# A fused attention, expert and dense kernel: results stored out of another tile, a third bank in the last layer, one more weight split early

## The chip, the cores and the metric

The kernel runs on one core of a Trainium2 chip. The metric is the device time of one execution in microseconds (us); for each kernel the median of several executions is given. A core has five engines that run their own instruction streams beside each other: PE (matrix products), DVE (vector), ACT (scalar), POOL (GpSimd) and SP (which here issues nearly all DMAs). They wait for each other by semaphores.

## The reference

```python
# 1. attention, 2 batches x 8 heads x 768 positions x 64, only between
#    positions whose query and key fall into the same of 64 hash buckets
# 2. experts: x is [1536, 512]; each token goes to 2 of 8 experts
h = np.maximum(x[mask] @ w1[e], 0.0)                 # w1 [8, 512, 1024]
out[mask] += top2_w[mask, k, None] * (h @ w2[e])     # w2 [8, 1024, 512]
# 3. dense layer
h = x @ w_in                                         # [512, 2048]
g = h - np.tanh(h)
return (g @ w_out).astype(np.float32)                # [2048, 512]
```

The result has shape [1536, 512]. The weights of the dense layer come in 64-bit form and are turned into float32 inside the kernel.

## The kernel before, in words

The attention fills the first third of the span; from there on PE does the products of the experts and of the dense layer.

**Products in parts.** Each operand of a product is split into a high part, which PE takes at its faster float type, and a low part, the remainder. A product is three matmuls: high by high, high by low, low by high (L1068 to L1070 for the first product of an expert, L1093 to L1095 for the second). `split_w` makes the parts of a weight tile `wt` out of a raw tile `wraw`: ACT copies the high part (L851), then the low part is a subtraction (L850), on POOL in two halves for experts 0, 1 and 7, on DVE in one piece for the others. In the last layer DVE does it in two halves, which wait in a list `later` and are taken out one by one around a step's other work.

**Segments.** `segs` lists the expert work: segments 0 and 1 are expert 0, one for each batch (240 rows of tokens, two row blocks of 120); segments 2 to 7 are experts 1 to 6 (448 rows, three blocks and a tail); segments 8 and 9 are expert 7 (240 rows each). The main loop goes over segments 1 to 9; a segment has eight steps f, one for each 128 columns of w1. In a step PE does the first product of the next step (`h_step`), ACT and DVE turn its bank into `hh` and `hl` (relu, high and low: L1084, L1086), and PE then does the second product of this step into banks that stay open over the whole segment (`y_step`). After the last step `y_out` copies these banks to a tile in SBUF (DVE L1125, ACT L1123), and the store to the DRAM tensor `Y` (L1126) goes out at the next `store()`.

**What holds the order.** The order on each engine is the one in which the code is written. In a step the loop does: `store()`; as many `fetch()` as the depth allows (a DMA from DRAM into a raw tile: L876 and L878 for experts, L874 from `W2f` for the dense layer); `load_x` (L1048, L1051: token rows of the next segment from `Xg`); `trans_x` (PE transposes the token rows L1061, ACT and DVE make high part `xh` and low part `xl`: L1062, L1063); and `next_w`, the split of one weight tile, in the steps that a table names (`LASTW` in the last segment).

**Tiles.** `stg` has two raw tiles `wraw`; a fetch or a result that wants one waits until the last reader of that tile is done. The tiles `xh` and `xl` of a segment come from `mx[n % 2]`: even and odd segments have one set each. The last layer's rows (block 0 to 3 of 384 rows) use the same two sets.

**The conditional.** In segment 1 all engines read a count (L1256) and jump past a block that handles experts with too many tokens (`tc.If`, L1257). With these inputs the block is not entered.

**The last layer.** It has 4 blocks of 16 steps. `h2_step` does the first product into a bank of group "b", ACT forms the square and the tanh (L1368 to L1375), POOL one subtraction (L1374), DVE three steps of a polynomial (L1379, L1381, L1383; the last one reads the bank and so frees it), a predicated copy (L1393) and the low part (L1399). `o2_step` does the second product. `combine` turns the next block's rows (L1350) into banks of group "a" and writes `xh` and `xl` (L1352, L1353); for block 0 this happens in the last segment. A bank is one of eight of 2 KB per partition; a product waits until the last reader of its bank is done.

Of the kernel before, what the change touches and what calls it, by code (L numbers as in the profile page):

```python
# [6 lines left out]
F32 = mybir.dt.float32  # L7
# [13 lines left out]
PF = 3  # L21
# [14 lines left out]
CAP = 448  # L36
# [4 lines left out]

LASTV = (0, 2, 3, 4, 5, 6)

LASTW = (2, 3, 5, 7)

WARM = (7, 1, 2, 10)

# [29 lines left out]
def body(tc, q, k, v, proj, w_gate, w_noise, noise, w1, w2, w_in, w_out, out):  # L77
    nc = tc.nc
    PS = bass.MemoryType.PSUM
    B, H, S, D = q.shape  # L80
# [4 lines left out]
    DM = H * D  # L85
    KD4 = DM // 128
# [13 lines left out]
    with ExitStack() as ctx:  # L100
# [6 lines left out]
        stg = pool("stg", 2)  # L107

        banks = dict(BANKS)
        nbank = dict.fromkeys(banks, 0)  # L110

        def bank(tag):
            r = banks[tag]
            nbank[tag] += 1
            n = r[nbank[tag] % len(r)]
            return psp.tile([128, 512], F32, tag=f"b{n}", name=f"bank{n}")
# [720 lines left out]
        rings = {}  # L837
# [24 lines left out]
        wsrc = [(e, f) for e in range(E) for f in range(NF)] + [("m", f) for f in range(NF2)]  # L862
        wn = [0]
        rings["A"] = wA

        fn, RAW = [0], {}
# [125 lines left out]
        for g in range(NI // 2):  # L992
# [14 lines left out]
            b, P = divmod(g, NP)  # L1007
# [27 lines left out]
        def blocks(n):  # L1035

            rows, nb = segs[n][3:]
            m = min(rows // nb, 128)
            return m, rows - nb * m
# [74 lines left out]
        def y_out(n):  # L1114
            e, b, r0, rows, nb = segs[n]
            m, tail = blocks(n)
            if nb == 2:
                yo = stg.tile([128, 2, DM], F32, name="wraw")
            else:
                yo = mm[n % len(mm)].tile([128, 4, DM], F32, name="xy")  # L1120
            for j, ps in enumerate(YP[n][:nb]):
                if j % 2:
                    nc.scalar.activation(yo[:m, j], ps[:m], AF.Copy)  # L1123
                else:
                    nc.vector.tensor_copy(yo[:m, j], ps[:m])  # L1125
            stores.append(lambda: nc.sync.dma_start(out=Y[r0:r0 + nb * m].rearrange("(p j) d -> p j d", j=nb), in_=yo[:m, 0:nb]))  # L1126
            if tail:
                ps = YP[n][nb]
                nc.scalar.activation(yo[:tail, nb], ps[64:64 + tail], AF.Copy)
                nc.vector.tensor_tensor(yo[:tail, nb], ps[:tail], yo[:tail, nb], op=ALU.add)  # L1130
                stores.append(lambda: nc.sync.dma_start(out=Y[r0 + nb * m:r0 + rows], in_=yo[:tail, nb]))
# [38 lines left out]
        mm, mx = {}, {}  # L1170
# [34 lines left out]
        last = NI - 1  # L1205
# [112 lines left out]
        BC = TB // 128  # L1318
# [22 lines left out]
        def combine(t0):  # L1341

            blk, j = divmod(t0, BC)
            if j == 0:
                XH2[blk] = mx[blk % 2].tile([128, KD4, CAP], F32R, name="xh")
                XL2[blk] = mx[blk % 2].tile([128, KD4, CAP], F32R, name="xl")
            u = hd["g", t0][:, 0]
            ps = bank("a")
            for dc in range(KD4):
                nc.tensor.transpose(ps[:, ck(dc)], u[:, ck(dc)], ident)  # L1350
            p3 = ps.rearrange("p (c n) -> p c n", c=KD4)
            nc.scalar.activation(XH2[blk][:, :, ck(j)], p3, AF.Copy)  # L1352
            later.insert(0, lambda: nc.vector.tensor_tensor(XL2[blk][:, :, ck(j)], p3, XH2[blk][:, :, ck(j)].bitcast(F32),  # L1353
                                                            op=ALU.subtract))
# [76 lines left out]
        NSG = len(segs)  # L1431
        for n in range(1, NSG):
            last = n == NSG - 1
            if n == NSG - B:
                rings["C2"] = ctx.enter_context(tc.tile_pool(name="wC2", bufs=WC2, reuse_waits="tile"))
                store()
                mid.close()
                del rings["st"]
                rings["C"] = ctx.enter_context(tc.tile_pool(name="wC", bufs=WC, side="right", reuse_waits="tile"))
            if last:  # L1440
                store()
                m2 = ctx.enter_context(tc.tile_pool(name="m2", bufs=2, side="right", reuse_waits="tile"))
                gb2 = m2.tile([128, 1], F32, name="gb2")
                nc.vector.memset(gb2, G2 / (2 * G3))
                gsb = m2.tile([128, 1], F32, name="gsb")
                nc.vector.memset(gsb, -GS)
            fx = 0 if n == B - 1 else 1
            for f in seg_steps(n, None if last else n + 1):
                if (n, f) == (1, IFS):
                    sched.close()  # L1450
                    overflow()
                    manual()
                store()
                while fn[0] < min(wn[0] + (PF if "st" in rings else 1), len(wsrc)):
                    fetch()
                if not last and f == fx:
                    load_x(n + 1)
                for dc in range(0 if last else KD4):
                    if f == (5 + dc // 2 if n == B - 1 else 3 + dc):
                        trans_x(n + 1, dc)  # L1460
                if (1, CV1 + 4) <= (n, f) < (NSG - B, 0):
                    convert_more(CVN)
                if (1, CV1) <= (n, f) < (NSG - B, 0):
                    while conv64 and len(RAW64) + (hd.get("cv") is not None) < 2:
                        fetch64(conv64.pop(0))
                if segs[n][1] in (None, B - 1) and (f in LASTW if last else n >= B or f >= W1) or n == NSG - B and f in LASTV:
                    next_w()
                if B <= n < B + WN0 - NF and f == 4:
                    next_w()
                for j in range(BC if last else 0):  # L1470
                    if f == 1 + j // 2:
                        gather(j)
                    if f == 4 + j:
                        combine(j)
                        flush(1)
                    if f == 3 + j:
                        mix(j)
                        flush(1)
        store()
        hd["second"] = True  # L1480
        done = -1
        for n in range(-LA, len(steps2)):
            la = LA + (LAE if n + LA >= len(steps2) - 2 else 0)
            while done < min(n + la, len(steps2)):
                done += 1
                h2_step(at(done), at(done - 1))
            blk, f = at(n + LA) or (NBK, 0)
            for j in range(BC if blk + 1 < NBK else 0):
                t0 = (blk + 1) * BC + j
                if f == 3 + 2 * j:  # L1490
                    gather(t0)
                if f == 9 + j:
                    mix(t0)
                if f == 11 + j:
                    combine(t0)
            if n >= 0:
                flush(max(0, len(later) - 2))
                next_w()
                o2_step(*steps2[n])
# [30 lines left out]
```

## Time and profile before

| | us |
|---|---|
| median of 3 runs | 928.76 |
| lowest and highest of the runs | 925.42, 929.61 |
| the profiled execution | 933.93 |
| its span | 932.1 |
| PE busy in it | 897.7 |

The span is what the trace covers; the profiled execution lasts 1.83 us longer than its span, and is 5.17 us above the median of the runs. In the rows further down, a time at the start of a row is in us from the start of the span. Square brackets at the end of a row tell how long the engine sat idle before that instruction and what ended the idle time: an engine, the tile, and the line; "SPq" and "ACTq" are an engine's own sequencer.

### The profile page before, as it was taken

Reading aid. Unit: us, or ns where it says so; the run is one execution under the profiler, and the core shown is the slowest. Engines: PE = TensorE matmul, PEld = TensorE weight load, DVE = VectorE, ACT = ScalarE, POOL = GpSimd, SP = SyncE. Lnnn points to the kernel's source line nnn. Section 1 sums busy time; section 2 is a strip of 40 time slices with the busy share of each in tenths; the row PEclk is TensorE's granted clock in tenths of the full one; section 3 lists DMA queues with packets and bytes.
Section 4 is the critical chain, followed back from the end, with each engine's and each line's share of the span. In section 5 each row is a group of like instructions: output and inputs, shape, how many; then the busy total and the mean of one; then the engine's idle time right before and its main releaser. Section 6 shows DMA issues by size and latency. Waiting matters only on the chain.

```text
span 932.1 us, 13632 instructions
## 1 busy us (share of the span) xinstructions
PE 897.7 (96%) x4736; PEld 699.3 (75%) x4736; DVE 677.7 (73%) x1290; ACT 539.9 (58%) x1039; POOL 372.8 (40%) x325
## 2 busy tenths in 40 slices
PE   8999999998997788999999999999999999999998
PEld 3555555554556677888888888888889899989997
DVE  7788787889757325797887878665888677677665
ACT  7658666864453133444444444454777777777765
POOL 6687778875667443000000004602342342342221
PEclk9999999999999899999999999999999999999999
DMA  5635553300222478686858777555420110110000
GB/s 123 171 117 170 159 182 106 103 24 7 93 64 95 163 222 256 218 287 214 271 199 292 236 255 248 174 197 179 135 69 1 57 46 1 57 46 1 35 1 34
DMA packets 104625, 123.72 MB, mean 133 GB/s; under 512 B 32121, under 2 KB 75177, under 8 KB 104553
## 3 DMA queue, kind: packets, MB, share of 16 engines
q1 hardware_dynamic: 100712, 110.23, 37.6%
q0 software_dynamic: 3840, 12.59, 4.0%
q8 instruction: 38, 0.62, 0.3%
q14 instruction: 35, 0.28, 0.1%
HBM read 82.79 MB, written 37.72 MB: 129 GB/s over the span
## 4 chain that ended last, share of the span: by engine, by line
PE 55%; DVE 3%; ACT 1%; DMA 1%; issue 1%; POOL 0%; DVEq 0%; SPq 0%; POOLq 0%
PE bank L1068 9%; PE bank L1070 9%; PE bank L1069 9%; PE bank L1095 8%; PE bank L1094 8%; PE bank L1093 8%; PE bank L1110 2%; PE bank L1061 1%; DVE g_u L1381 1%; PE bank L1350 1%; DMA xy<-Xg 1%; DVE wt L850 1%; DMA Y<-xy 0%; DVE hh L1399 0%; DVE g_u L1383 0%
## 5 line engine op out<-in xcount | busy, mean ns | idle before, releaser
L1068 PE MATMUL bank<-xh,wt 128*128 128x384 f32 (+2 forms) x544 | 186.3, 342 | 4.8 <-DVE g_u L1383 2.8
L1069 PE MATMUL bank<-xl,wt 128*128 128x384 f32 (+2 forms) x544 | 183.1, 337 | 0.0
L1070 PE MATMUL bank<-xh,wt 128*128 128x384 f32 (+2 forms) x544 | 183.1, 337 | 0.0
L1093 PE MATMUL bank<-wt,hh 128*128 128x512 f32 (+1 forms) x400 | 159.6, 399 | 9.5 <-ACT hh L1084 6.1
L850 POOL TENSOR_TENSOR wt<-wraw,wt 128x512 fp32r<-128x512 f32 x48 | 68.5, 1451 | 246.8 <-ACT wt L851 234.7
L1095 PE MATMUL bank<-wt,hh 128*128 128x512 f32 (+1 forms) x400 | 159.3, 398 | 0.1
L1094 PE MATMUL bank<-wt,hh 128*128 128x512 f32 (+1 forms) x400 | 158.9, 397 | 0.0
L1374 POOL TENSOR_TENSOR g_th<-g_h,g_th 128x384 f32<-128x384 f32 x64 | 67.2, 1050 | 187.2 <-ACT g_th L1373 186.7
L450 ACT ACTIVATE p<-bank 128x384 f32<-128x384 f32 x192 | 91.8, 489 | 72.1 <-PE bank L449 66.1
L415 DVE TENSOR_REDUCE mx<-bank 128x1 f32<-128x384 f32 x192 | 103.3, 551 | 31.1 <-PE bank L414 29.0
L1068 PEld LDWEIGHTS bank<-xh,wt 128*128 128x128 f32 x544 | 102.5, 188 | 13.9 <-DVE g_u L1383 4.8
L1069 PEld LDWEIGHTS bank<-xl,wt 128*128 128x128 f32 x544 | 102.5, 188 | 6.7 <-DVE xl L1353 0.2
L851 ACT ACTIVATE wt<-wraw 128x1024 fp32r<-128x1024 f32 x80 | 84.2, 1054 | 36.4 <-PE bank L1110 20.5
L1070 PEld LDWEIGHTS bank<-xh,wt 128*128 128x128 f32 x544 | 102.4, 188 | 3.1
L1093 PEld LDWEIGHTS bank<-wt,hh 128*128 128x128 f32 (+1 forms) x400 | 75.6, 189 | 22.9 <-ACT hh L1084 6.4
L483 POOL TENSOR_TENSOR ps<-ps,p 128x768 f32<-128x768 f32 x47 | 85.9, 1827 | 11.7 <-ACT p L450 7.1
L1095 PEld LDWEIGHTS bank<-wt,hh 128*128 128x128 f32 (+1 forms) x400 | 75.5, 189 | 18.3 <-DVE hh L1399 0.6
L1084 ACT ACTIVATE hh<-bank 128x448 fp32r<-128x448 f32 (+1 forms) x80 | 37.7, 473 | 83.6 <-PE bank L1070 34.9
L1086 DVE SCALAR_TENSOR_TENSOR hh<-bank,hh 128x384 fp32r<-128x384 f32 (+2 forms) x128 | 45.8, 388 | 54.7 <-ACT hh L1084 46.0
L1094 PEld LDWEIGHTS bank<-wt,hh 128*128 128x128 f32 (+1 forms) x400 | 75.5, 189 | 12.8
L474 PE MATMUL bank<-p,v 128*64 128x384 f32 x384 | 83.8, 515 | 0.0
L448 PE MATMUL bank<-qc,kb 108*128 108x384 f32 (+1 forms) x192 | 79.2, 412 | 1.8 <-DVE qc L438 1.6
(250 smaller groups left out, 1629.4 us busy)
## 6 DMA issues: line engine op xcount, KB each, us to landing
wraw<-in_moe_w_dram SPq DMA_DIRECT2D x128, 256.0 KB
cv_t<-in_moe_w_in_dram SPq DMA_DIRECT2D x16, 512.0 KB
cv_t<-in_moe_w_out_dram SPq DMA_DIRECT2D x16, 512.0 KB
W2f<-cv_w SPq DMA_DIRECT2D x16, 512.0 KB
wraw<-W2f SPq DMA_DIRECT2D x16, 512.0 KB
Xg<-zero SPq DMA_DIRECT2D x14, 512.0 KB
Y<-zero SPq DMA_DIRECT2D x9, 512.0 KB
xy<-Xg SPq DMA_DIRECT2D x6, 768.0 KB
```

The costliest lines, as they stand in the source:

```text
L415: nc.vector.tensor_reduce(MX[i % 2][:, c, hf:hf + 1], ps[:, :HF], op=ALU.max, axis=AX.X)
L448: nc.tensor.matmul(ps[:, :HF], KB[sn(g, par)][r, ck(kc)], QC[sn(g, par)][r, half(hf)], start=True, stop=False)
L450: nc.scalar.activation(hd["p", i, kc][:, half(hf)], ps[:, :HF], AF.Exp, scale=float(D) ** -0.5)
L474: nc.tensor.matmul(hd["o", i][hf * D:(hf + 1) * D, :HF], raw["v", g][:, par, kc], hd["p", i, kc][:, half(hf)], start=(kc == 0), stop=(kc = ...
L483: eng.tensor_tensor(t, hd["p", i, 0] if kc == 1 else t, hd["p", i, kc], op=ALU.add)
L851: nc.scalar.activation(t[:, 0], r, AF.Copy)
L1068: nc.tensor.matmul(ps[:, :n], ws(0, dc), xh[:, dc, :n], start=(dc == 0), stop=False)
L1069: nc.tensor.matmul(ps[:, :n], ws(0, dc), xl[:, dc, :n], start=False, stop=False)
L1070: nc.tensor.matmul(ps[:, :n], ws(1, dc), xh[:, dc, :n], start=False, stop=(dc == KD4 - 1))
L1093: nc.tensor.matmul(ps[:m], a, t[:, 0, 1], start=first, stop=False)
L1094: nc.tensor.matmul(ps[:m], a, t[:, 1, 1], start=False, stop=False)
L1095: nc.tensor.matmul(ps[:m], l, t[:, 0, 1], start=False, stop=last)
```

## The change

There are five edits:

1. `y_out` of a segment with two row blocks (0, 1, 8 and 9) no longer takes a raw tile from `stg`. It takes the buffer of the segment's own low part, `xl` of `mx[n % 2]`, of which the last reader is the segment's last first product.
2. `LASTW` names one more step, 6, so that five weight tiles of the last layer are split in the last segment, and one fewer in the last layer's first block.
3. In the last segment the fetch depth is 2 instead of 1 from step 3 on.
4. In segment 8 the token rows of segment 9 are transposed at steps 4, 5, 6, 6 instead of 3, 4, 5, 6.
5. In the last layer, group "a" is bank 1 and group "b" banks 2, 3 and 0, until the first `combine` of that layer (block 1's, row tile `t0 == BC`); from there "a" is banks 0 and 1 and "b" banks 2 and 3, as before.

```diff
-LASTW = (2, 3, 5, 7)
+LASTW = (2, 3, 5, 6, 7)
...
             if nb == 2:
-                yo = stg.tile([128, 2, DM], F32, name="wraw")
+
+                yo = mx[n % 2].tile([128, KD4, CAP], F32, name="xl")
+                yo = yo.rearrange("p c n -> p (c n)")[:, 0:2 * DM].rearrange("p (j d) -> p j d", j=2)
...
-                while fn[0] < min(wn[0] + (PF if "st" in rings else 1), len(wsrc)):
+                while fn[0] < min(wn[0] + (PF if "st" in rings else 2 if last and f >= 3 else 1), len(wsrc)):
                     fetch()
...
-                    if f == (5 + dc // 2 if n == B - 1 else 3 + dc):
+                    if f == (5 + dc // 2 if n == B - 1 else min(4 + dc, 6) if n == NSG - 2 else 3 + dc):
                         trans_x(n + 1, dc)
...
         hd["second"] = True
+
+        banks.update(a=[1], b=[2, 3, 0])
+        nbank["b"] %= 2
...
                 if f == 11 + j:
+                    if t0 == BC:
+                        banks.update(a=[0, 1], b=[2, 3])
+                        nbank.update(a=0, b=min(nbank["b"] % 3, 1))
                     combine(t0)
```

The lines behind `y_out` stand two lines further down in the changed kernel (the store L1126 is L1128 there, the jump L1257 is L1259).

**SP around the conditional, in segments 0 and 1.** `wraw` are the weight fetches, `xy<-Xg` the loads of token rows, `Y<-` the store of segment 0's result. Before:

```order
L878 DMA wraw<-in_moe_w_dram 128x512
L1256 TENSOR_LOAD cmi
L1256 ISA x2
L1048 DMA xy<-Xg 120x1024
L876 DMA wraw<-in_moe_w_dram 128x4x128
L1126 DMA Y<-wraw 120x1024
L878 DMA wraw<-in_moe_w_dram 128x512
L1048 DMA xy<-Xg 128x1536
L1051 DMA xy<-Xg 128x512
L876 DMA wraw<-in_moe_w_dram 128x4x128
L878 DMA wraw<-in_moe_w_dram 128x512
L1257 COMPARE_AND_BRANCH
```

After:

```order
L878 DMA wraw<-in_moe_w_dram 128x512
L876 DMA wraw<-in_moe_w_dram 128x4x128
L878 DMA wraw<-in_moe_w_dram 128x512
L876 DMA wraw<-in_moe_w_dram 128x4x128
L878 DMA wraw<-in_moe_w_dram 128x512
L1258 TENSOR_LOAD cmi
L1258 ISA x2
L1048 DMA xy<-Xg 120x1024
L1048 DMA xy<-Xg 128x1536
L1128 DMA Y<-xl 120x1024
L1051 DMA xy<-Xg 128x512
L1259 COMPARE_AND_BRANCH
```

Two weight fetches, of two DMAs each, that stood behind the reading of the count now stand ahead of it; between the load of token rows and the store of the result no weight fetch is left.

**DVE in the first steps of the last layer** (numbers behind names tell buffers apart; `bank3_7244` is a tile in bank 3). Before, the fourth and fifth step with a split in two halves:

```order
L1383 SCALAR_TENSOR_TENSOR g_u_7212<-g_u_7212,bank2_7196 128x384
L1393 COPY_PREDICATED g_u_7212<-g_m_7213,g_th_7211 128x384
L850 TENSOR_TENSOR wt_7233<-wraw_7231,wt_7233 128x512
L1399 TENSOR_TENSOR hh_7263<-g_u_7212,hh_7263 128x384
L850 TENSOR_TENSOR wt_7233<-wraw_7231,wt_7233 128x512
L1379 SCALAR_TENSOR_TENSOR g_u_7260<-g_u_7260,g_s_7257 128x384
L1381 SCALAR_TENSOR_TENSOR g_u_7260<-g_u_7260,g_s_7257 128x384
L1383 SCALAR_TENSOR_TENSOR g_u_7260<-g_u_7260,bank3_7244 128x384
L1393 COPY_PREDICATED g_u_7260<-g_m_7261,g_th_7259 128x384
L850 TENSOR_TENSOR wt_7279<-wraw_7277,wt_7279 128x512
L1399 TENSOR_TENSOR hh_7309<-g_u_7260,hh_7309 128x384
L850 TENSOR_TENSOR wt_7279<-wraw_7277,wt_7279 128x512
```

After, the same two steps from the copy on, and the head of the next:

```order
L1395 COPY_PREDICATED g_u_7217<-g_m_7218,g_th_7216 128x384
L850 TENSOR_TENSOR wt_7238<-wraw_7236,wt_7238 128x512
L1401 TENSOR_TENSOR hh_7268<-g_u_7217,hh_7268 128x384
L850 TENSOR_TENSOR wt_7238<-wraw_7236,wt_7238 128x512
L1381 SCALAR_TENSOR_TENSOR g_u_7265<-g_u_7265,g_s_7262 128x384
L1383 SCALAR_TENSOR_TENSOR g_u_7265<-g_u_7265,g_s_7262 128x384
L1385 SCALAR_TENSOR_TENSOR g_u_7265<-g_u_7265,bank3_7249 128x384
L1395 COPY_PREDICATED g_u_7265<-g_m_7266,g_th_7264 128x384
L1401 TENSOR_TENSOR hh_7310<-g_u_7265,hh_7310 128x384
L1381 SCALAR_TENSOR_TENSOR g_u_7307<-g_u_7307,g_s_7304 128x384
L1383 SCALAR_TENSOR_TENSOR g_u_7307<-g_u_7307,g_s_7304 128x384
L1385 SCALAR_TENSOR_TENSOR g_u_7307<-g_u_7307,bank0_7291 128x384
```

The fifth pair of L850 is gone from the last layer, and the polynomial's last step (L1385, before L1383) goes on from bank 3 to bank 0, where before it went from bank 3 back to bank 2.

## Rows read from the trace of the kernel before

**Rows 1.** Waits of PE, whole span: us in total, times, longest us.

```profile
PE bank L1093 <- ACT hh L1084: 6.1, 2, 5.1
...
PE bank L1068 <- DVE g_u L1383: 2.8, 5, 1.0
PE bank L1093 <- DVE wraw L1125: 2.8, 1, 2.8
...
PE bank L1061 <- DMA xy<-Xg: 0.5, 1, 0.5
```

**Rows 2.** Windows: length, busy (instructions) per engine, granted clock, DMA share, GB/s.

```profile
420.00:600.00 180.00, 180.00 (x870) 156.65 (x869) 139.73 (x197) 80.57 (x109) 21.21 (x13) 1.00 0.74 243
```

**Rows 3.** Timeline of PE: start, us, line, shapes, idle before and releaser.

```profile
333.92 0.38 PE L1068 MATMUL bank<-xh,wt 128*128 128x240 f32 x1 [1.98 <-ACTq L1257]
344.72 0.50 PE L1093 MATMUL bank<-wt,hh 128*120 128x512 f32 x1 [0.93 <-ACT hh L1084]
359.88 0.47 PE L1093 MATMUL bank<-wt,hh 128*128 128x512 f32 x1 [2.80 <-DVE wraw L1125]
```

**Rows 4.** Timeline of ACT in segment 1: high parts of weight splits.

```profile
332.51 1.06 ACT L851 ACTIVATE wt<-wraw 128x1024 fp32r<-128x1024 f32 x1 [4.32 <-DMA wraw<-in_moe_w_dram]
343.35 1.06 ACT L851 ACTIVATE wt<-wraw 128x1024 fp32r<-128x1024 f32 x1 [3.55 <-DMA wraw<-in_moe_w_dram]
355.38 1.06 ACT L851 ACTIVATE wt<-wraw 128x1024 fp32r<-128x1024 f32 x1 [3.96 <-DMA wraw<-in_moe_w_dram]
```

**Rows 5.** Timeline of SP: issues of fetches and of two stores.

```profile
310.96 0.39 SPq L876 DMA_DIRECT2D wraw<-in_moe_w_dram  x1
327.33 0.35 SPq L1126 DMA_DIRECT2D Y<-wraw  x1
339.54 0.39 SPq L876 DMA_DIRECT2D wraw<-in_moe_w_dram  x1
345.07 0.47 SPq L876 DMA_DIRECT2D wraw<-in_moe_w_dram  x1
...
631.21 0.35 SPq L1126 DMA_DIRECT2D Y<-wraw  x1
```

**Rows 6.** Waits of SP between 300 and 365 us, same columns as group 1.

```profile
SPq L1257 <- SPq L1257: 5.3, 1, 5.3
```

**Rows 7.** POOL and DVE at the end of segment 1.

```profile
356.52 2.49 POOL L850 TENSOR_TENSOR wt<-wraw,wt 128x512 fp32r<-128x512 f32 x2 [4.51 <-ACT wt L851]
...
359.05 0.69 DVE L1125 COPY wraw<-bank 120x512 f32<-120x512 f32 x1 [1.45 <-POOL wt L850]
```

**Rows 8.** Windows around the clock's fall and the busy DMA stretch, columns as group 2.

```profile
340.00:356.00 16.00, 15.07 (x94) 13.27 (x93) 3.78 (x8) 6.42 (x11) 9.68 (x8) 1.00 0.97 316
...
361.10:364.50 3.40, 3.40 (x10) 2.74 (x9) 3.33 (x6) 1.88 (x3) 2.77 (x2) 0.50 0.94 236
364.50:367.90 3.40, 3.40 (x18) 2.99 (x17) 3.24 (x4) 1.15 (x2) 0.98 (x1) 1.00 0.75 238
```

**Rows 9.** Timeline of PE: an early step of the last layer.

```profile
657.25 0.45 PE L1068 MATMUL bank<-xh,wt 128*128 128x384 f32 x1 [0.99 <-DVE g_u L1383]
```

**Rows 10.** DVE, one step with a split to the next.

```profile
674.76 0.60 DVE L1393 COPY_PREDICATED g_u<-g_m,g_th 128x384 f32<-128x384 uint32 x1
...
679.67 0.60 DVE L1393 COPY_PREDICATED g_u<-g_m,g_th 128x384 f32<-128x384 uint32 x1
```

**Rows 11.** Windows: last segment, last layer after the splits; columns as group 2.

```profile
625.00:655.00 30.00, 30.00 (x194) 26.57 (x193) 16.31 (x27) 14.65 (x26) 6.98 (x6) 1.00 0.54 168
...
695.00:725.00 30.00, 30.00 (x157) 27.16 (x156) 24.74 (x44) 24.05 (x51) 7.47 (x8) 1.00 0.00 1
```

**Rows 12.** Windows around the stall ahead of segment 1, columns as group 2.

```profile
316.73:323.56 6.83, 4.67 (x13) 3.70 (x14) 2.55 (x11) 1.37 (x4) 0.00 (x0) 0.50 0.22 87
...
310.00:318.00 8.00, 3.22 (x18) 2.51 (x18) 1.26 (x6) 0.26 (x1) 4.87 (x5) 0.92 0.89 277
```

**Rows 13.** DVE: the last layer's first writer of a low part tile.

```profile
644.89 0.69 DVE L1353 TENSOR_TENSOR xl<-bank,xh 128x512 fp32r<-128x512 f32 x1 [1.67 <-ACT xh L1352]
```

## The prediction

> **What bounds the kernel now.** I read the waits of PE first, then windows, then the timelines of the engines that PE waited for. PE is the bound: over the whole of 420 to 600 us it is busy 180.00 of 180 us [rows 2], so nothing that is taken off another engine there can pay. What the change can win lies in PE's waits [rows 1]: 2.80 us for the copy of a result into a raw tile, two waits for `hh` of together 6.1 us (5.1 and so 1.0 us; the timeline shows the second as 0.93), five in the last layer of together 2.8 us, 0.5 us for token rows, and 1.98 us behind the conditional [rows 3]. These, without the 5.1, are 9.0 us, about 1% of the span.
>
> **Early fetches (edit 1), around the conditional.** The DMA of a raw tile at 310.96 is followed on SP by the store of segment 0's result at 327.33, and only then come the second half of that fetch and the next fetch [rows 5]. ACT therefore gets the raw tile late: its split at 332.51 waited 4.32 us for the DMA, the `hh` that PE needs stands behind it, and PE waits until 333.92 [rows 3, 4]. In the changed order these fetches stand ahead of the reading of the count, and need only a free raw tile. The result no longer occupies one, so I expect them out before 310 us. The split is then ready long before PE asks. Of the 1.98 us I take 1.8 as gain and leave 0.2 for the conditional itself (bounds 1.6 and 2.0).
>
> The next wait, 0.93 us at 344.72, hangs on the split at 343.35, which waited 3.55 us for a DMA that SP issued at 339.54 [rows 3 to 5], that is after its jump past the conditional, on which SP stood 5.3 us [rows 6]. The jump starts when POOL and ACT have done the split that was late; that split was held for 4.32 us on ACT and can now start when ACT is free; I estimate that the jump and all fetches behind it move by 3 us, against 1.8 us for PE. So the wait goes if the fetch chain gains more than PE: 0.9 us (bounds 0.5 and 0.9).
>
> **A rule beside it.** SP's own wait at the jump is 5.3 us with the DMA engines filling up [rows 6, 8]. The Trainium skill says, in "Runtime: NRT & Kernel Launch", section "Instruction fetch mechanics", that a taken branch whose target lies outside the pages at hand makes the engine fetch the target by DMA before it goes on. By that rule the jump would get shorter when fewer weight DMAs are under way, as here after the change, and the next term would come out at its upper end, 2.8 instead of 2.3, the sum at 8.8; by the row alone, with 5.3 us kept, it stays at 8.3.
>
> **The result's tile (edit 1), end of segment 1.** At 359.88 PE waited 2.80 us for DVE's copy of the result at 359.05; that copy, 0.69 us, itself waited for POOL's two halves of a split, 356.52 plus 2.49 us, since its target was the raw tile that POOL still read [rows 3, 7]. With the low-part tile as target this wait is gone. What is late next is the split itself: ACT's 355.38 waited 3.96 us for the DMA issued at 345.07 [rows 4, 5]; that tile took 10.3 us to arrive in a stretch with a DMA share of 0.97 [rows 8]. If the whole chain of fetches moves 3 us earlier with the jump, it arrives near 352 and PE is 2.7 us earlier, so little is left of the wait. Gain 2.3 (bounds 1.8 and 2.8).
>
> **The clock.** From 361.10 to 364.50, right behind the wait of 2.80, the granted clock is 0.50, which is 1.2 GHz, and PE does 10 matmuls; in the 3.40 us after that, at 1.00 (2.4 GHz), 18 [rows 8]. So the low stretch costs 3.40 x (1 - 10/18) = 1.5 us. The waits of 1.98 and 0.93 us were not followed by such a stretch, a remaining wait under 1 us should not be either. Gain 1.5 (bounds 0 and 1.5).
>
> **Later transposes (edit 4).** The 0.5 us for token rows [rows 1] goes, as PE asks a step later. Steps 6 and 6 now hold two transposes together, whose `xh` and `xl` come just ahead of their first use; I charge 0.2 for it. Gain 0.3 (bounds 0 and 0.5).
>
> **Last layer (edits 2, 3 and 5).** A DVE step with a split takes 679.67 - 674.76 = 4.91 us [rows 10]. PE's own step is 21 matmuls; at 157 in 30.00 us [rows 11] that is 4.0 us. So in those five steps DVE is the bound and PE waits: 0.99 at 657.25 [rows 9], then four of 0.44 to 0.48, together 2.8 [rows 1]. Moving one split out takes one slow DVE step away, 0.45 by the waits and 0.9 by the two step times; I take 0.7. The third bank lets PE run one product further ahead of DVE's last read; it covers the first wait, 0.99, all but some 0.2, but not the later ones, since the second product still waits for `hl`, behind the same DVE work. That gives 0.8, together 1.5 (bounds 0.7 and 2.8). The split itself goes to the last segment, where ACT is busy 14.65 and DVE 16.31 of 30.00 us [rows 11]; its 1.06 us on ACT [rows 4] and its subtraction on DVE are covered there; without that cover the 1.06 us would be added. The deeper fetch (edit 3) is what makes it come in time; on SP it stands ahead of the last segment's store, with no one waiting for that store until the next block's rows are gathered. I cost it at nothing.
>
> **The sum.** 1.8 + 0.9 + 2.3 + 1.5 + 0.3 + 1.5 = 8.3 us. Against the profiled execution, 933.93, that is 925.6. It lies 5.2 above the median of the runs, 928.76; nothing in the terms depends on that difference, so the median becomes 928.76 - 8.3 = 920.5. The lower bounds add to 1.6 + 0.5 + 1.8 + 0 + 0 + 0.7 = 4.6, the upper to 2.0 + 0.9 + 2.8 + 1.5 + 0.5 + 2.8 = 10.5; not all will lie at one end, so the forecast's own range is 918.3 to 924.2.
>
> **Rival 1: the DMA stretch keeps its own time.** From 340 to 356 us the DMA share is 0.97 at 316 GB/s [rows 8]. If what arrives there is limited by bytes and not by when SP issues, the raw tile of 355.38 still lands at 355.3. PE then gets there earlier and waits longer, the 1.8 and 0.9 are given back, and of the 2.80 only the wait for the raw tile's release goes: DVE's copy could start at about 358.3 instead of 359.05, 0.8 us. The low clock stays. The gain is 0.8 + 0.3 + 1.5 = 2.6, the time 926.2. For it speaks the share of 0.97; against it that ACT waited for single tiles, which were issued late, and that two fetches leave the time just ahead of that stretch for a much earlier one. Chance 0.18.
>
> **Rival 2: the stall before the conditional shrinks too.** PE's largest wait in this part is 5.1 us for `hh` [rows 1], followed by 6.83 us at a clock of 0.50 with PE busy 4.67 [rows 12]. The fetch at 310.96 [rows 5] falls into a stretch with a DMA share of 0.89 and leaves it in the changed order. If the stall came from that crowd, up to 5.1 + 4.67/2 = 7.4 us go as well: 913.1; half of it gives 916.8. Against it: 256 KB at 277 GB/s [rows 12] are 0.9 us, far less than the stall. Chance 0.07, at 915.
>
> **Rival 3, on the other side: the store holds the next writer of the low-part tile.** The result now leaves from `xl`, and the next that writes this buffer must wait until the store has read it. In the last layer that is DVE's 644.89 [rows 13], 13.7 us behind the store at 631.21 [rows 5], and PE's first product of that layer stands behind it. A raw tile in the crowded stretch took 10.3 us to arrive. So the mechanism begins to cost from a landing of 13.7 us; to use up the whole gain and 4.6 us more it must land 13.7 + 8.3 + 4.6 = 26.6 us after its issue, and the time is then over 933.4. Against it: the crowd there is thinner, with a DMA share of 0.54 [rows 11]. Chance 0.05, at 935.
>
> **Chances.** The forecast has 0.70, the rivals 0.18, 0.07 and 0.05. About 0.5%, 4.6 us, is what a measurement of this kernel can tell from no change: faster means below 924.1, slower above 933.4. Faster: of the forecast nearly all, 0.66, and rival 2, 0.07, together 0.73. Slower: rival 3 and what I haven't seen, 0.06. The rest, 0.21, is within. The range for 8 in 10 takes the forecast's own range and rival 1: 916.0 to 926.2.
>
> **What will show it.** In the changed trace: the two fetches issued before 305 us and PE without a wait of over 0.5 us near 332; SP's next fetch after the jump at 337 or earlier; PE's second product of segment 2 without a wait for a copy; no window at 0.50 between 355 and 365; in the last layer four pairs of split halves with PE waits of together 1.0 to 1.6 us. The prediction is wrong if a raw tile still lands at 355, if the low clock returns elsewhere, or if a wait on `xl` or on the store appears in PE's list.

## The result, and the profile after

| | before | after |
|---|---|---|
| median of 6 runs, us | 929.56 | 920.08 |
| lowest and highest | 925.42, 930.57 | 917.76, 922.01 |
| the profiled execution, us | 933.93 | 921.54 |
| its span, us | 932.1 | 919.7 |

The ratio is 0.9907 with a 95% interval of 0.9884 to 0.993, so the change saves 8.6 us (6.5 to 10.8) of 929.56. The forecast was 920.5 us, with a gain of 8.3 us.

The waits of PE in the changed kernel, to be held against [rows 1] (us in total, times, longest):

```profile
PE bank L1093 <- DVE xl L1127: 1.4, 1, 1.4
PE bank L1061 <- DMA xy<-Xg: 1.2, 1, 1.2
PE bank L1093 <- ACT hh L1396: 1.2, 4, 0.3
...
PE bank L1069 <- DVE xl L1063: 0.6, 1, 0.6
```

The 6.1 us for `hh`, the 2.0 behind the conditional and the 2.8 for the polynomial's last step are gone. Half of the 2.8 us for the result's copy is left (L1127 now), the last layer has four small waits for `hh`, and there is a new wait for a low part (L1063). The 1.2 us for token rows is at segment 1, not at segment 9.

The timeline of PE at the places of [rows 3], and at the new wait:

```profile
326.51 0.35 PE L1068 MATMUL bank<-xh,wt 128*128 128x240 f32 x1
...
349.88 0.47 PE L1093 MATMUL bank<-wt,hh 128*128 128x512 f32 x1 [1.38 <-DVE xl L1127]
...
616.68 0.38 PE L1069 MATMUL bank<-xl,wt 128*128 128x240 f32 x1 [0.59 <-DVE xl L1063]
```

The first row is the matmul that waited 1.98 us at 333.92 before. It starts without a wait. What held the fetches before is in SP's waits between 326 and 334 us: the store stood 15.9 us for DVE's copy of the result, with every later issue behind it, and the next fetch stood 1.0 us for that store to land, since both use a raw tile:

```profile
SPq L1126 <- DVE wraw L1125: 15.9, 1, 15.9
SPq L876 <- DMA Y<-wraw: 1.0, 1, 1.0
```

The timeline of SP in the changed kernel:

```profile
297.42 0.37 SPq L876 DMA_DIRECT2D wraw<-in_moe_w_dram  x1
...
299.85 0.37 SPq L876 DMA_DIRECT2D wraw<-in_moe_w_dram  x1
...
330.14 0.40 SPq L876 DMA_DIRECT2D wraw<-in_moe_w_dram  x1
```

The two fetches that moved go out at 297.42 and 299.85, ahead of the store, and the first fetch behind the jump at 330.14 instead of 339.54 [rows 5]. That is 9.4 us earlier in the trace, while PE's matmul behind the conditional is 7.4 us earlier (326.51 against 333.92): the fetches gained 2.0 us on PE.

**One trace of before is not enough to size this.** The profiled execution before was 4.4 us above the median of the runs. Two more traces of the unchanged kernel were taken, and with them the next section measures in this way: the same matmul is looked up in two traces, and the difference of its two starts is its lag; how the lag changes from one place to the next tells what was won or lost between them. The first of them, `e0_before`, has no stall and no low clock in the places of interest, so it is the zero line. Its largest waits behind the attention part:

```profile
PE bank L1093 <- DVE wraw L1125: 3.2, 1, 3.2
PE bank L1068 <- DVE g_u L1383: 2.8, 5, 1.0
...
PE bank L1061 <- DMA xy<-Xg: 1.9, 2, 1.1
PE bank L1093 <- ACT hh L1084: 1.7, 1, 1.7
...
PE bank L1068 <- ACTq L1257: 1.6, 1, 1.6
```

The wait of 5.1 us in segment 0 [rows 1] is not there, nor, at that place, in any of the other 12 traces taken. It belongs to that one execution, with the low clock behind it [rows 12].

### The profile page after: what moved, and what is told of

It reads as the page before. It is cut to its first block, busy times and chain, and to the rows that moved or that the text cites. A ratio compares the mean times of both kernels' runs of the same rounds, so it can differ in the third digit from the quotient of the medians.

```text
span 919.7 us, 13620 instructions
## 1 busy us (share of the span) xinstructions
PE 894.9 (97%) x4736; PEld 697.2 (76%) x4736; DVE 678.0 (74%) x1289; ACT 540.3 (59%) x1039; POOL 372.0 (40%) x325
## 4 chain that ended last, share of the span: by engine, by line
PE 56%; DVE 3%; DMA 2%; ACT 1%; issue 1%; SPq 0%; POOL 0%; DVEq 0%
PE bank L1069 9%; PE bank L1070 9%; PE bank L1068 9%; PE bank L1095 9%; PE bank L1094 9%; PE bank L1093 9%; PE bank L1110 2%; PE bank L1061 1%; DMA wraw<-W2f 1%; DMA wraw<-in_moe_w_dram 1%; DVE wt L850 1%; DVE g_u L1383 1%; PE bank L1352 1%; DMA Y<-xy 0%; DVE g_u L1395 0%
## 5 line engine op out<-in xcount | busy, mean ns | idle before, releaser
L850 POOL TENSOR_TENSOR wt<-wraw,wt 128x512 fp32r<-128x512 f32 x48 | 67.9, 1437 | 234.1 <-ACT wt L851 224.8
```

## The experiments

Change of lag against `e0_before`, in us, worked out from the starts of the same matmuls; negative is earlier. The columns are places in the time of `e0_before`: around the conditional (324 to 326), the following `hh` (326 to 338), the end of segment 1 with what follows it (338 to 370), token rows of segment 9 and its first product (604 to 622), segment 9 (622 to 646), the start of the last layer (646 to 650), the rest (650 to the end).

| kernel | conditional | next hh | end of seg. 1 | rows of seg. 9 | seg. 9 | last layer, start | rest |
|---|---|---|---|---|---|---|---|
| before, first trace | 0.39 | -0.77 | 1.19 | -0.57 | 0.01 | 0.01 | -0.08 |
| before, third trace | 0.07 | -0.48 | 1.63 | -0.59 | -0.02 | 0.00 | -0.02 |
| changed | -1.48 | -1.94 | -1.78 | -0.17 | 0.06 | -1.28 | -0.14 |
| edit 1 alone | -1.47 | -1.94 | -2.50 | 0.06 | -0.03 | 0.00 | -0.02 |
| edit 1, segment 0 alone | -1.47 | -1.94 | -1.42 | 0.01 | 0.00 | 0.00 | -0.04 |
| edit 1, segment 1 alone | 0.25 | -0.74 | -2.45 | -0.59 | 0.00 | 0.00 | -0.06 |
| edits 2 to 5 | 0.93 | -0.44 | -1.35 | -1.03 | 0.05 | -1.28 | -0.16 |
| edit 4 alone | 1.63 | -0.95 | -1.05 | -0.27 | 0.01 | 0.00 | -0.08 |
| edits 2, 3, 5 | 0.01 | -0.71 | -0.19 | -0.33 | 0.06 | -1.28 | -0.14 |
| edit 5 alone | 1.64 | -0.97 | -1.35 | -0.37 | 0.02 | -1.28 | 0.60 |
| pair of transposes early | -1.47 | -1.94 | -2.64 | -1.13 | -0.04 | -1.28 | -0.14 |
| changed without edit 3 | -1.40 | -1.94 | -2.74 | -0.70 | 0.06 | -1.28 | 5.22 |
| six splits | -1.47 | -1.94 | -2.98 | -0.97 | 1.83 | -1.28 | -0.86 |

Rows without edit 1 differ among themselves by up to 3.0 us in a place that their edit does not touch; rows with it in segment 0 agree to 0.1 us in the first two places. The zero line itself, not shown in the table, is one such execution: at the end of segment 1 three of the other kernels without edit 1 are 1.05 to 1.35 us better than it, so a single entry there is no proof of a gain. The times of the runs are each held against executions of the kernel before that were taken together with them; the medians of those were 929.56, 928.24, 926.40 and 926.76 us.

**The kernel before again.** No edit.

> The kernel before, unchanged, for a second trace. Theory 1 (the 5.1 us stall of PE ahead of the conditional belongs to the one execution that was profiled, as the runs without a profile are 4.4 us shorter than that execution): PE's list of waits has no wait of about 5 us for hh in segment 0, and the span is 926 to 928 us. Theory 2 (the stall is in every execution of the kernel before, and the change removed it): the wait of 5 us for hh is there again, span 930 to 933 us.

Measured: 925.54 us, no wait of 5 us. Theory 1 holds, though the span, 923.8 us, is even shorter than its 926 to 928. The stall showed in one of the three traces of this kernel, and in none of the five others that read the count with the fetches still behind it; it is no fixed part of the time that an edit could remove, and rival 2 of the prediction has nothing to explain in the medians.

> The kernel before once more for its trace. Theory 1: the stall of 5.1 us is not there, the wait behind the conditional is 1.6 to 2.7 us, with a stretch of low clock behind it where it is over 2 us and none where it is under. Theory 2 (the stall is in a large share of executions): it is there again.

Measured: 926.88 us, no stall, a wait of 1.7 us behind the conditional with no low clock behind it. But the clock fell elsewhere, behind the 3.2 us wait for the result's copy. Windows of the third trace of before and, second, of `e0_before` (columns as in [rows 2]):

```profile
353.00:356.40 3.40, 3.40 (x9) 2.70 (x10) 2.81 (x5) 2.85 (x4) 1.80 (x2) 0.54 0.79 184
```

```profile
353.00:356.40 3.40, 3.40 (x17) 2.96 (x16) 3.11 (x5) 2.55 (x4) 2.10 (x2) 1.00 0.91 222
```

Both kernels are the same, both waited 3.2 us just ahead of that window, and one has a granted clock of 0.54 behind it with 9 matmuls, the other 1.00 with 17. So a wait of this length may be followed by the low clock or not.

**Edit 1 alone, and all but edit 1.**

```diff
 # edit 1 alone: against the kernel before
             if nb == 2:
-                yo = stg.tile([128, 2, DM], F32, name="wraw")
+                yo = mx[n % 2].tile([128, KD4, CAP], F32, name="xl")
+                yo = yo.rearrange("p c n -> p (c n)")[:, 0:2 * DM].rearrange("p (j d) -> p j d", j=2)
```

> Edit 1 alone: results of segments 0, 1, 8 and 9 go into the low-part tile, everything else as before. Theory 1: the terms that the trace of the changed kernel shows for this edit, 2.2 at the wait behind the conditional, 1.1 at the next, 1.5 at the copy of segment 1's result and 1.6 for the low clock, together 6.4 us, so 923.2 us against 929.6. Theory 2 (the stall of 5.1 us and its low clock go with this edit too): 11 to 13 us, 917 to 918 us. Rival 1 of the prediction (the DMA stretch keeps its own time): 0.8 us, 928.8 us.

Measured: 920.86 us against 928.24, ratio 0.992 (0.99 to 0.9939), 7.4 us (5.7 to 9.3).

> The changed kernel with edit 1 undone: edits 2 to 5 alone. Theory 1: the last layer gains 1.2, the later transposes cost 0.4 by the trace of the changed kernel (they were forecast to gain 0.3), together 0.8 us, 928.8 us. The prediction's terms give 1.8 us, 927.8 us. Theory 2 says nothing else here, the stall stays.

Measured: 925.57 us, ratio 0.9976 (0.9965 to 0.9988), 2.2 us (1.1 to 3.2). The two parts add up to 9.6, inside the interval of the whole. Edit 1 is about three quarters of them. The 2.2 us lie above the 0.8 of Theory 1 and agree with the 1.8 of the prediction's terms. Theory 2 wanted 11 to 13 us of it and falls with the interval; rival 1 of the prediction wanted 0.8 and falls too.

**Edit 1 in one segment.**

```diff
-            if nb == 2:
+            if nb == 2 and not (n == 0):
                 yo = stg.tile([128, 2, DM], F32, name="wraw")
+            elif nb == 2:
+                yo = mx[n % 2].tile([128, KD4, CAP], F32, name="xl")
...
```

> Edit 1 for segment 0 alone; segments 1, 8 and 9 store out of a raw tile as before. Theory 1: the fetches around the conditional are early, 2.2 + 1.1 = 3.3 us are gained, but the copy of segment 1's result waits for a raw tile again, so the 1.5 and the 1.6 of the low clock are not: 926.3 us. Rival 1: nothing is gained, since the DMA stretch behind the conditional keeps its time, 929.0 us or more. Theory 2: 8 to 9 us, 921 us, if it is the early fetch that removes the stall.

Measured: 922.47 us, ratio 0.9945 (0.9925 to 0.9966), 5.1 us (3.2 to 7.0). The first two columns carry 1.47 and 1.94 us, exactly as with the whole edit, so the early fetches are what wins them. So rival 1's 0 falls, and so do the 8 to 9 us of Theory 2; the 3.3 us of Theory 1 lie just inside the interval. Nothing is given back in the crowded stretch behind it. The wait for the result's copy, whose cause was left in, is 1.8 us:

```profile
PE bank L1093 <- DVE wraw L1128: 1.8, 1, 1.8
```

That is less than the 3.2 of the zero line, but no sign of the edit: with edits 2 to 5 and with edit 5 alone, both with late fetches, it is 1.8 us too.

> Edit 1 for segment 1 alone; segments 0, 8 and 9 store out of a raw tile as before, so the fetches around the conditional are late. Theory 1 (what ends the wait at the end of segment 1 is first the raw tile's landing, then its release): the copy of segment 1's result no longer waits for POOL, but the split and the hh before it still wait for the late DMA; of a wait of 1.8 to 3.2 us 0.5 to 0.8 go, 927 to 928 us where the kernel before has 927 to 928.5. Rival (the release of the raw tile alone sets that wait, as the profile's row names it): 1.8 to 2.8 us gained at that place and the wait is gone from PE's list.

(The edit is the one above with `n == 1`.) Measured: 924.29 us against 926.76, ratio 0.9972 (0.9958 to 0.9985), 2.6 us (1.4 to 3.9). The place gains 2.45 us against the zero line with the fetches as late as before, far more than the 0.5 to 0.8 that Theory 1 left for the release. PE's waits keep the conditional and lose most of the copy:

```profile
PE bank L1068 <- ACTq L1260: 1.9, 1, 1.9
...
PE bank L1093 <- DVE xl L1128: 0.7, 1, 0.7
```

How much of the 2.45 is the tile's release, and how much the landing of the next raw tile, ACT's split and DVE's copy tell, in `e0_before` and then with segment 1's edit:

```profile
347.96 1.06 ACT L851 ACTIVATE wt<-wraw 128x1024 fp32r<-128x1024 f32 x1 [4.37 <-DMA wraw<-in_moe_w_dram]
351.61 0.69 DVE L1125 COPY wraw<-bank 120x512 f32<-120x512 f32 x1 [1.45 <-POOL wt L850]
```

```profile
346.73 1.06 ACT L851 ACTIVATE wt<-wraw 128x1024 fp32r<-128x1024 f32 x1 [3.42 <-DMA wraw<-in_moe_w_dram]
348.86 0.68 DVE L1128 COPY xl<-bank 120x512 f32<-120x512 f32 x1
```

PE's wait for the copy is shorter than ACT's wait for the raw tile, by 1.13 to 1.18 us in each of the eight traces in which segment 1's result goes into a raw tile (4.37 and 3.21 us in `e0_before`), and by 2.70 to 2.72 in each of the six in which it goes into the low-part tile (3.42 and 0.72 here). The release is therefore worth 1.5 us whenever the tile lands, about the 1.45 us for which DVE stood idle behind POOL. The rest is the landing, for which ACT waits 2.96 to 4.40 us from trace to trace in the kernels without edit 1. So both theories have a part: the landing ends the wait for the split, and the release comes on top of it with twice what Theory 1 gave it.

**Later transposes.**

```diff
-                    if f == (5 + dc // 2 if n == B - 1 else 3 + dc):
+                    if f == (5 + dc // 2 if n == B - 1 else min(4 + dc, 6) if n == NSG - 2 else 3 + dc):
```

> Edit 4 alone, the transposes of segment 9 at steps 4, 5, 6, 6. Theory 1: PE's wait for the token rows (0.5 us in the first trace of the kernel before, 1.1 in the second) goes, and a wait of some 0.4 us for the last pair's low part comes: a gain of 0.1 to 0.7 us, 927.5 to 928.1 us against 928.2. Rival: the wait that comes is as long as the wait that goes, no difference in the trace at the end of segment 8.

Measured: 926.56 us against 926.4, ratio 1.0006 (0.9993 to 1.0019): no difference. In the trace the wait for token rows goes, 1.49 us against a zero line that waits 1.1 us, and at the first product of segment 9 PE stands for the low part of the pair:

```profile
620.51 0.38 PE L1069 MATMUL bank<-xl,wt 128*128 128x240 f32 x1 [0.63 <-DVE xl L1063]
```

In this trace the wait and the two transposes ahead of it cost 1.2 us, and against the first and third trace of before, where the token rows are late by 0.5 us only, the edit loses 0.3 us. But other traces with the same edit differ: with edits 2 to 5 PE has no wait for the low part and the column shows 1.03 us gained on the zero line. What decides is a landing again. The pair's low part stands on DVE behind a split, and that split behind ACT's, which waits for a raw tile. ACT in the changed kernel, and with edits 2 to 5:

```profile
613.67 1.06 ACT L851 ACTIVATE wt<-wraw 128x1024 fp32r<-128x1024 f32 x1 [1.14 <-DMA wraw<-W2f]
```

```profile
616.51 1.06 ACT L851 ACTIVATE wt<-wraw 128x1024 fp32r<-128x1024 f32 x1 [0.53 <-DMA wraw<-W2f]
```

Over the four traces with this edit ACT waits 0.53, 0.88, 1.14 and 1.18 us there, and PE 0, 0.34, 0.59 and 0.63 for the low part. The column is -0.54 in their mean, and -0.30 in the mean of the eight traces with the transposes as before: the edit gains about 0.2 us.

> The changed kernel with the transposes of segment 9 at steps 4, 5, 5, 6, so that the pair does not stand last. Theory 1: the new wait for the low part at the start of segment 9 goes, 0.4 to 0.9 us less than the changed kernel in the trace at that place, 919 us, 9 to 10 us under the kernel before. Rival: DVE is so full in that step that the pair delays hh there and the wait only moves, the same time as the changed kernel.

```diff
-                    if f == (5 + dc // 2 if n == B - 1 else min(4 + dc, 6) if n == NSG - 2 else 3 + dc):
+                    if f == (5 + dc // 2 if n == B - 1 else (4, 5, 5, 6)[dc] if n == NSG - 2 else 3 + dc):
```

Measured: 917.87 us against 926.4, ratio 0.991 (0.9895 to 0.9924), 8.3 us (7.0 to 9.7). In the trace PE no longer waits for the low part, and the place gains 1.13 us instead of 0.17, that is 1.0 us more than the changed kernel and 0.6 us more than the mean of the four traces with the pair last. The intervals of the runs don't tell the two kernels apart.

**The last layer.**

```diff
 # all three edits; edit 5 alone is the last five lines
-LASTW = (2, 3, 5, 7)
+LASTW = (2, 3, 5, 6, 7)
...
-                while fn[0] < min(wn[0] + (PF if "st" in rings else 1), len(wsrc)):
+                while fn[0] < min(wn[0] + (PF if "st" in rings else 2 if last and f >= 3 else 1), len(wsrc)):
...
+        banks.update(a=[1], b=[2, 3, 0])
+        nbank["b"] %= 2
...
+                    if t0 == BC:
+                        banks.update(a=[0, 1], b=[2, 3])
+                        nbank.update(a=0, b=min(nbank["b"] % 3, 1))
```

> Edits 2, 3 and 5, the last layer's alone. Theory 1: 1.2 to 1.5 us gained, 926.9 us, PE's waits for the polynomial's last step (2.8 us) gone and waits of together 1.0 to 1.2 us for hh in their place, four of them. Rival: the last layer is bound by DVE's work alone and nothing is gained by the bank, 0.5 to 0.7 us for the one split that moved.

Measured: 925.17 us against 926.4, ratio 0.9988 (0.9979 to 0.9997), 1.1 us (0.3 to 1.9); in the trace 1.28 + 0.14 = 1.42 us, with four waits for `hh` of together 1.1 us. The interval holds the rival's 0.5 to 0.7 too; the trace speaks for Theory 1.

> Edit 5 alone, the third bank, with all five splits still in the last layer. Theory 1 (the bank takes the first wait of 0.99 and adds slack that the later steps use up): 0.8 us gained, 927.4 us, five waits of about 0.3 us for hh behind DVE. Rival (PE waits for the second product's operand as long as it waited for the bank): 0 to 0.3 us gained, the five waits of together 2.8 us turn into waits for hh of together over 2.3 us.

Measured: 926.59 us, ratio 0.9998 (0.9986 to 1.0009), not told from no change; in the trace 1.28 us won at the start, of which 0.60 is given back in the steps with splits, 0.68 us in all. PE's waits, first with edits 2, 3 and 5, then with the bank alone:

```profile
PE bank L1093 <- ACT hh L1397: 1.1, 4, 0.3
```

```profile
PE bank L1093 <- ACT hh L1397: 1.4, 5, 0.3
```

As Theory 1 had it, the wait for the bank (2.8 us in five) has become a shorter wait for `hh`, one for each split that is left in the last layer. By the difference, 1.42 - 0.68, the split that moved out is worth 0.74 us.

> The changed kernel with edit 3 undone: fetch depth 1 in the last segment, with five splits there. Theory 1: the fifth raw tile comes too late for its step, ACT stands in the split with the next hh behind it, and PE waits some 1 to 3 us in the last segment: 921 to 923 us where the changed kernel has 920. Rival: the depth covers nothing, the same time as the changed kernel.

```diff
-                while fn[0] < min(wn[0] + (PF if "st" in rings else 2 if last and f >= 3 else 1), len(wsrc)):
+                while fn[0] < min(wn[0] + (PF if "st" in rings else 1), len(wsrc)):
```

Measured: 925.05 us against 926.76, ratio 0.9985 (0.9973 to 0.9998): of the gain 1.4 us are left. I had the place and the size wrong: the last segment is undisturbed, and the loss, 5.2 us, is in the last layer. ACT, PE, and a window behind them:

```profile
645.54 1.06 ACT L851 ACTIVATE wt<-wraw 128x1024 fp32r<-128x1024 f32 x1 [6.03 <-DMA wraw<-W2f]
```

```profile
651.00 0.79 PE L1093 MATMUL bank<-wt,hh 128*128 128x512 f32 x1 [5.70 <-ACT hh L1396]
```

```profile
647.00:654.00 7.00, 3.00 (x7) 2.42 (x8) 5.66 (x10) 5.21 (x11) 2.18 (x2) 0.58 0.22 76
```

The split of step 7 finds its raw tile only just asked for: its fetch went out behind segment 9's store. ACT waits 6.03 us in it, the square and the tanh of the last layer's first steps stand behind it, PE waits 5.70 us and then runs at a granted clock of 0.58 in that window. Edit 3, which has no gain of its own, carries this.

> The kernel with the pair of transposes at step 5 and one more split in the last segment, at step 4, so six there and three pairs left in the last layer. Theory 1: each step with a split costs PE 0.3 to 0.7 us in the last layer, so 0.4 to 0.7 us are gained once more if the last segment covers the split: 917.2 us where the kernel with five has 917.9. Rival: six splits and the fetches for them do not fit into the last segment, ACT or the landing holds hh there, and PE waits: 918 to 921 us.

```diff
-LASTW = (2, 3, 5, 6, 7)
+LASTW = (2, 3, 4, 5, 6, 7)
```

Measured: 919.92 us, ratio 0.9923 (0.9906 to 0.9941), 7.1 us (5.5 to 8.7). The last layer gains 0.86 instead of 0.14 behind its start, 0.72 us for one more split, the same as for the fifth; but segment 9 loses 1.83 us. The split delays DVE's weighting of the rows, and PE waits for it:

```profile
PE bank L1352 <- DVE xy L1341: 1.5, 2, 1.0
```

The time is in the rival's range, though PE's wait is for these rows and not for `hh`.

## Why the prediction was right, point by point

The terms, in us. The first measured column takes the mean of the three traces of before (the zero line included) against the trace of the changed kernel. The second takes all traces: for the first three rows the seven kernels without edit 1 against the five with it in both segments, for the transposes the eight without edit 4 against the four with it, for the last layer the seven with none of its edits against the four with all three.

| term | forecast | measured | measured, all traces |
|---|---|---|---|
| behind the conditional | 1.8 | 0.15 + 1.48 = 1.6 | 2.1 |
| next `hh` | 0.9 | -0.42 + 1.94 = 1.5 | 1.3 |
| end of segment 1, and the clock | 2.3 + 1.5 = 3.8 | 0.94 + 1.78 = 2.7 | 2.4 |
| later transposes | 0.3 | -0.39 + 0.17 = -0.2 | 0.2 |
| last layer | 1.5 | -0.03 + 1.42 = 1.4 | 1.4 |
| sum | 8.3 | 7.0 | 7.4 |

The sums by traces lie inside the interval of the runs, 6.5 to 10.8; where the 1.2 to 1.6 us up to the runs' 8.6 come from is open. The places and the order of size are right. That 8.3 came within 0.3 us of 8.6 is luck: one term is too large by 1.1 to 1.4 us, and the next `hh` too small by 0.4 to 0.6.

**Early fetches.** Right in mechanism and place: one segment's edit gives both terms alone. The second was sized too small. I had read it off the one wait of 0.93 us; in the other traces of before the same wait was 1.2 and 1.7 us. One reading was wrong: the jump of SP did not start when the late split was done. SP's last issue ahead of it ended at 332.88, while ACT was still in that split, from 332.51 to 333.57 [rows 4]. SP was held by the store and its landing. Its last issue ahead of the jump, before and in the changed kernel:

```profile
331.72 1.16 SPq L878 DMA_DIRECT2D wraw<-in_moe_w_dram  x1
```

```profile
322.05 0.39 SPq L1051 DMA_DIRECT2D xy<-Xg  x1
```

It ends 10.4 us earlier, and PE's matmul behind the conditional starts 7.4 us earlier.

**The jump.** The rule quoted from the Trainium skill ("Runtime: NRT & Kernel Launch", section "Instruction fetch mechanics") is that a taken branch to a target outside the pages at hand waits for a DMA fetch. From it I took that the jump might get shorter with fewer DMAs under way, and set this beside the forecast, which kept 5.3 us. It did not get shorter. In the three traces of before SP stands 5.2 to 5.4 us at it, in the changed kernel this long:

```profile
SPq L1259 <- SPq L1259: 6.8, 1, 6.8
```

Over all 14 traces it is 4.7 to 5.5 us with the late fetches and 4.7 to 6.8 with the early ones, so it has not clearly changed. That a fetch belongs to this jump agrees with the traces: in each of them four packets go through an instruction queue, q14, while SP stands there, the first 2.7 to 4.3 us after it began. Before (332.9 to 338.5 us) and in the changed kernel (322.4 to 329.3), with packets, MB and share of the 16 engines:

```profile
q14 instruction: 4, 0.03, 1.6%
```

```profile
q14 instruction: 4, 0.03, 1.2%
```

What fewer DMAs would do is not tested: although the weight fetches had left, the DMA share where the jump begins was 0.93 (321.5 to 325.5 us) against 0.94 before (332 to 336).

**The result's tile.** The release of the raw tile was a cause, as forecast, but the 2.3 us were argued wrongly. I let the raw tile arrive 3 us earlier and PE come 2.7 us earlier, and concluded that little of the wait would be left. What is left is the difference of the two: ACT still waits 4.09 us for the tile in the changed kernel, 3.36 in the mean of the five with edit 1 in both segments, and 3.74 in the mean of the seven without it. So 0.4 us come from the landing and 1.5 from the release, 1.9 together, and PE's wait for the copy is not gone (1.38 us).

**The clock.** Of the terms this one was sized worst. I tied the low stretch at 361.10 [rows 8] to the wait of 2.80 us ahead of it and counted its 1.5 us in full. Of three traces of before it stands behind that wait in two, and in one with 3.2 us it doesn't; nor does it with edits 2, 3 and 5, where PE waits 3.0 us. With edits 2 to 5, edit 4 or edit 5 alone it stood instead behind the wait at the conditional, 2.5 to 2.7 us there, three times. So five of the seven traces without edit 1 have one such stretch between 320 and 370 us, and none of the seven with edit 1 in one or both of the segments has one. That it goes with the waits is borne out. A gain of this kind has to be counted by how often it comes, here some 1 us by my estimate (five in seven, at 1.5), of which only 0.4 falls to the end of segment 1.

**Later transposes.** The forecast of 0.3 us agrees with the 0.2 of all traces, but the changed kernel's own trace shows a loss, and the runs of edit 4 alone tell neither from nothing. The charge of 0.2 us for the pair is between 0 and 0.6 us, as the raw tile ahead of it lands.

**The last layer.** Both parts were sized rightly: the bank 0.8 forecast, 0.7 in the trace; the split 0.7 forecast, 0.7 in the trace. That the waits would turn into waits for the second product's operand is what the changed trace shows. The cover that I named for the fifth split was the right one, with a wrong price: without the deeper fetch it costs 5.2 us in the one trace taken, not 1.06.

**The rivals.** Rival 1 fell as a whole with segment 0's edit alone. One thing in it is right: ACT waits nearly as long for the raw tile as before. Its price for the release was too small, 0.8 us from a copy at 358.3; no row gives that time, and DVE was free from 357.60, 1.45 us ahead of its copy [rows 7]. Rival 2 has no object in the medians, the stall being in one execution only; what made that execution stall stays open. Rival 3 did not show: no engine waits for a store out of the low-part tile in the changed trace.

**The signs named ahead.** Both fetches, PE at the conditional, SP's next fetch, the clock between 355 and 365 us and the last layer came as named. PE's second product of segment 2 still waits for a copy. And by its letter one sign of being wrong is there: PE's list has two waits on `xl`, 1.4 us for the result's copy, which now writes there, and 0.6 us for the low part of segment 9's rows. Neither is the wait for a store that the sign was meant for.

## What to carry to other kernels

A buffer that fetches and results share couples two queues: a store that waits for its data keeps back every fetch behind it on the same queue, and a copy into the buffer waits for the last reader of a weight. Giving the result a tile that is dead by then cuts both, and no cost of it showed here. When an edit puts work into a fuller stretch, look first whether its input can be asked for one step sooner; that decided between a gain of 0.7 us and a loss of 5.2. And before a wait of one trace is turned into a term, take a second trace of the same kernel, and of the changed one before its sign is called wrong.

## What the runs showed of the hardware

The granted clock does not follow from the length of a wait alone. In the attention part PE waits 1.4 us for DVE (L414) near 231 us in every trace taken. The wait in `e0_before`, and the ten us behind it (columns as in [rows 2]):

```profile
231.79 0.44 PE L414 MATMUL bank<-kb,qc 96*128 96x384 f32 x1 [1.38 <-DVE mx L415]
```

```profile
231.00:241.00 10.00, 8.61 (x46) 4.66 (x47) 9.35 (x25) 3.40 (x7) 5.70 (x4) 1.00 0.03 13
```

The same in the changed kernel:

```profile
231.24 0.44 PE L414 MATMUL bank<-kb,qc 96*128 96x384 f32 x1 [1.39 <-DVE mx L415]
```

```profile
231.00:241.00 10.00, 9.35 (x37) 5.13 (x38) 8.26 (x20) 2.21 (x5) 4.45 (x4) 0.66 0.00 0
```

The same code behind the same wait runs at a granted clock of 1.00 in three of the 14 traces, at a mean of 0.83 in three and of 0.66 in eight (part of the ten us at 0.50, the rest at 1.00), and the lag between 228 and 245 us grows by about 0, 0.5 to 0.8, and 1.8 to 2.5 us with it. So a wait of 1.4 us was followed by the low clock in eleven traces, while behind waits of 3.0 and 3.2 us at the end of segment 1 the clock stayed at 1.00 in two. A single trace of this kernel is uncertain by about 2 us in a place that no edit touched, which is as much as most of the terms above.
